# The first stage of a spectral-mixing and GeGLU kernel: where the layer norm's statistics, tile 13, the reciprocal roots and the angle tables are done

## The chip, the cores and the metric

The program runs on one core of one Trainium2 chip. A core has five engines with an instruction queue each: TensorE (PE in the profile, with PEld for its weight loads), VectorE (DVE), ScalarE (ACT), GpSimd (POOL) and SyncE (SP), which issues most DMAs. Each engine takes its own instructions strictly in the order of its queue and waits on semaphores for the others. The metric is the device time of one execution in microseconds (us), lower is better, given as the median of several runs.

## The reference

One input `x` of 2048 rows by 576 columns goes through two residual blocks:

```python
x  = A_x
h  = x + irfft2(rfft2(layernorm(x)) * (w_r + 1j * w_i))     # over both axes
h2 = h + (gelu(layernorm(h) @ w_gate) * (layernorm(h) @ w_up)) @ w_down
```

`layernorm` subtracts the mean over the 576 columns and divides by the root of the variance plus 1e-5. `w_r` and `w_i` are 2048 x 289, `w_gate` and `w_up` 576 x 4608, `w_down` 4608 x 576. Inputs and output are bf16.

## The kernel before, in words

The 2048 rows lie as 16 tiles of 128 rows (`h_sb[:, h, :]`, h = 0 to 15), loaded by six DMAs (tiles 0-1, 2-3, 4-5, 6-7, 8-11, 12-15). The Fourier transforms are matrix products with tables of sines that the kernel makes itself. The second block, the feed-forward part (lines 876 to 910), is one long run of matrix products from about 73 us to the end. This case is about the first stage, the first 34 us or so.

The order on every engine is written out by hand: the program sits under `tc.manual_schedule()`, so each engine gets its instructions in the order of the source text. Waits between engines are put in where data or buffers need them.

The first stage does the following, and the names are those of the code:

- **Statistics of a tile.** Even tiles and tile 15 have theirs on DVE, `sd(h)` (L117 to L119): `bn_stats` over each half of 288 columns, then `bn_aggr`, which makes mean and variance of the two. Tiles 1, 3, 5, 7, 9, 11 and 13 have theirs on ACT, `ln_act(h)` (L124): two passes over the tile with an accumulated sum, one for the mean and one for the mean square. `ln_fin` (L128, L129, POOL) makes a variance of the latter.
- **Reciprocal roots.** `ln_rstd` (L133, L134) on POOL, for four tiles at a time: add 1e-5, then raise to the power -0.5.
- **Normalise and transform.** `norms(lo, hi)`: for each tile DVE writes `xn` (L137, one `tensor_scalar`), and `row16(h)` has PE multiply it with the row table `F16` (L298; for tiles up to 11 also L311, which tiles 12 to 15 do together later). `fill` (L286) is PE work without use, ahead of tiles 0, 8 and 12 (14, 8 and 5 matmuls of 512 columns).
- **Evictions.** `evict(h)` (L322) copies two tiles' products from PSUM to `Bt` on ACT; 14 and 15 go one by one. `evict4(h)` (L328) copies four tiles' last columns, on ACT, and for tiles 12 to 15 on DVE. Large PSUM tiles come from a ring of four (`two`).
- **Column tables.** `phases` (L268) and `drop_sign(kd, pd)` (L223) on DVE make the angles of the table `DT`; `col_sin(1, pd)` and `col_sin(0, kd)` (L347) on ACT take their sines. `DF` is cleared by POOL (L387) and filled from `DT` by two DVE copies (L427, L428).
- **Middle tables.** `angle_a` (L236), `angle_b` (L246, L247) and `angle_c` (L223) on DVE, then `sine` (L253) and `cosine` (L256) on ACT, `minus_sine` (L259) on DVE, make the table `TF`. It is done in two parts: `first` (2 of 9 blocks, 256 columns) and `rest` (7 blocks, 896 columns). A transposing DMA turns `TF` into `TI`.
- **On POOL beside this**: two gathering DMAs of the spectral weights, `wm_r` and `wm_i` (L381), and the clearing of `DI` (L399) and of three tiles `Zt` (L401).

Then the second stage begins: `f2(c)` on PE (L478) multiplies `Bt` with `DT` and `DF`, ACT copies the product out as `pq` (L486; for c = 9 DVE does), `f3` (L493, L494) multiplies `pq` with `TF`, ACT copies `g` and `hs` (L514), and DVE makes sums `xab` (L523, L524), products with the weights (L541, L547, L548) and `Zt` (L552, L553), which PE's `i3` (L569, L571) takes. This repeats for eight values of k. On ACT's queue `sine(rest)` stands ahead of the copy of the first `pq`.

Of the kernel before, what the change touches and what calls it, by code (L numbers as in the profile page):

```python
# [9 lines left out]
ACT = mybir.ActivationFunctionType  # L10
# [31 lines left out]
def kernel_body(  # L42
# [143 lines left out]
    iota(q16[:], [[16, P]])  # L186
# [10 lines left out]
    for t in range(3):  # L197
# [10 lines left out]
    fs = tmp("fs", [P, P], FP32)  # L208
    A.activation(
        fs[:], mu[:].rearrange("p c l -> p (c l)"), ACT.Sin, bias=npib[:], scale=2.0 * PI / P  # L210
    )
    ia, s2a, s2p = tmp("ia", [P, 1]), tmp("s2a", [P, 1], FP32), tmp("s2p", [P, 1], FP32)
    V.tensor_scalar(ia[:], ip[:], 7, None, op0=ALU.bitwise_and)
    V.tensor_scalar(s2a[:], ia[:], 127.0 / 8.0, None, op0=ALU.mult)
    V.scalar_tensor_tensor(s2p[:], ip[:], 0.125, s2a[:], op0=ALU.mult, op1=ALU.add)
    ks = tmp("ks", [P, 9], FP32)
    V.tensor_scalar(ks[:], kv[:], s2p[:, 0:1], None, op0=ALU.mult)
    V.tensor_scalar(iu[:], iu[:], 7, None, op0=ALU.bitwise_and)
    mask = tmp("mask", [P, P], FP32)
    V.tensor_scalar(mask[:], iu[:].rearrange("p c l -> p (c l)"), 0.0, None, op0=ALU.is_equal)  # L220
# [24 lines left out]
    def angle_b(sl):  # L245
        V.tensor_scalar(pr[:, sl], pr[:, sl], 2047, None, op0=ALU.bitwise_and)  # L246
        V.tensor_scalar(ab[:, sl], pr[:, sl], -1024.0, None, op0=ALU.add)  # L247
# [18 lines left out]
    def phases():  # L266
        for t in range(3):
            V.scalar_tensor_tensor(  # L268
                pd[:, t, :], iJ[:], iD[:, t : t + 1], kd[:, t, :], op0=ALU.mult, op1=ALU.add
            )  # L270

    def row_table():
        V.tensor_tensor(
            F16[:, 0:2, :],
            fs[:].unsqueeze(1).to_broadcast([P, 2, P]),
            mask[:].unsqueeze(1).to_broadcast([P, 2, P]),
            ALU.mult,
        )
        V.tensor_scalar(F16[:, 2, :], F16[:, 0, :], -1.0, None, op0=ALU.mult)
# [8 lines left out]
    def row16(h):  # L288
        if h % 2 == 0 or h == H - 1:
            ps_f[h] = two("f2t")  # L290
        if h % 4 == 0:
            ps_f["f4", h] = two("f4")
        f2t, b = (ps_f[h], 0) if h in ps_f else (ps_f[h - 1], 1)
        fill(f2t[:, b, :], {0: 14, 8: 8, 12: 5}.get(h, 0))
        x = xn[:, h, :]
        for t in range(2):
            for n, d0 in ((0, t * P), (1, DH + t * P)):
                T.matmul(  # L298
                    f2t[:, b, t * 2 * P : (t + 1) * 2 * P],
                    lhsT=x[:, d0 : d0 + P],  # L300
                    rhs=F16[:, n : n + 2, :],
                    start=(n == 0),
                    stop=(n == 1),
                )
        if h < 12:
            row16_rest(h)
# [25 lines left out]

    def sd(*hs):
        for h in hs:
            ln_dve(mv, h)
# [24 lines left out]
    sd(2)  # L360
    ln_fin(slice(1, 4, 2))
    ln_rstd(rstd, mv, 0, 4)
    sd(4, 6)
    norms(0, 4)
# [9 lines left out]
    angle_a(first)  # L374
    angle_b(first)
    angle_c(first)
    sine(first)
# [9 lines left out]
    G.memset(DF[:], 0.0)  # L387
    ln_fin(slice(9, 12, 2))
    sd(8, 10)
# [3 lines left out]
    ln_act(13)  # L393
    sd(12, 14)
    norms(8, 12)
    sd(15)
    ln_fin(slice(13, 14))
    ln_rstd(rstd, mv, 12, 16)
# [248 lines left out]
    for i in range(n + 1):  # L647
# [3 lines left out]
        if i == 0:  # L651
            f2(order[0] + 8)
            angle_c(rest)
            minus_sine(rest)
# [307 lines left out]
```

## Time and profile before

| what | time |
|---|---|
| median of 3 runs | 503.44 us (503.3 to 503.62) |
| the profiled execution | 503.36 us |
| its span in the profile | 501.3 us |
| PE busy | 491.3 us, 98% of the span |
| DVE busy | 211.3 us, 42% |
| ACT busy | 152.6 us, 30% |
| POOL busy | 28.5 us, 6% |

The span runs from the first to the last instruction; the 2.06 us between it and the execution's own time lie around the program. A line of the timeline gives the start in us from the span's beginning, the busy time, engine, source line, operation, the output `<-` inputs with shapes, how many instructions were merged, and in brackets the idle time before it with what ended it. On DVE a following instruction that needs nothing of the one before starts a little before that one's recorded end; one that does need it starts about 0.03 us after the end. PE is nearly full over the whole span, but the first 34 us are where its holes are.

### The profile page before, as it was taken

The numbers are of one execution on the slowest core, as the hardware profiler recorded it, in microseconds if no ns is written. First come the engines' busy times: TensorE is split into PE (matmuls) and PEld (weight loads), VectorE is DVE, ScalarE is ACT, GpSimd is POOL, SyncE is SP. The second block draws the span as 40 slices with busy tenths as digits, with TensorE's granted clock in tenths as the row PEclk, the third lists the DMA queues.
The fourth block names the chain that finished last, engine by engine and source line by source line (L and its number), as shares of the span: only waits on it lengthen the run. The fifth ranks groups of instructions, "written<-read, shape, count | busy, mean of one in ns | idle before, by whom it ended". The sixth has DMA issues, their size and how long they took to land.

```text
span 501.3 us, 9901 instructions
## 1 busy us (share of the span) xinstructions
PE 491.3 (98%) x4340; PEld 290.9 (58%) x4340; DVE 211.3 (42%) x420; ACT 152.6 (30%) x269; POOL 28.5 (6%) x75
## 2 busy tenths in 40 slices
PE   7999999999999999999999999999999999999996
PEld 3567765555567754444477744444677544444775
DVE  8999766788640125433310145333210233333001
ACT  8999972222320012323200032333100133232000
POOL 8500010111110000000000000000000000000000
PEclk9999999999999999999999999999999999999999
DMA  8539686799950049998800099988300688870000
GB/s 283 172 72 198 183 236 160 152 168 189 178 102 1 1 107 184 193 190 155 158 9 0 7 210 203 195 159 151 74 0 1 144 159 159 154 143 1 12 13 26
DMA packets 88104, 61.46 MB, mean 123 GB/s; under 512 B 22781, under 2 KB 86653, under 8 KB 88061
## 3 DMA queue, kind: packets, MB, share of 16 engines
q1 hardware_dynamic: 87773, 59.65, 60.2%
q0 software_dynamic: 288, 1.18, 0.7%
q8 instruction: 34, 0.56, 0.5%
q14 instruction: 9, 0.07, 0.0%
HBM read 52.65 MB, written 2.36 MB: 110 GB/s over the span
## 4 chain that ended last, share of the span: by engine, by line
PE 93%; DVE 3%; ACT 2%; POOL 1%; issue 0%; POOLq 0%
PE gu L876 56%; PE acc L896 28%; PE cs_ps L618 2%; PE pq_ps L478 2%; PE y_ps L741 1%; PE eo_ps L571 1%; PE eo_ps L569 1%; PE gh_ps L494 1%; DVE xn L137 1%; ACT cwb L631 1%; PE gh_ps L493 1%; PE f2t L298 0%; ACT DT L347 0%; ACT Bt L322 0%; POOL kd L198 0%
## 5 line engine op out<-in xcount | busy, mean ns | idle before, releaser
L876 PE MATMUL gu<-Bt,wgu 64*128 64x512 bf16 x2592 | 281.5, 376 | 0.8 <-ACT cwb L631 0.8
L876 PEld LDWEIGHTS <-wgu 64*128 64x128 bf16 x2592 | 130.9, 94 | 148.2 <-issue 1.8
L884 ACT ACTIVATE g_sb<-gu 128x512 f32<-128x512 f32 x144 | 86.0, 597 | 302.8 <-PE gu L876 302.8
L885 DVE TENSOR_TENSOR P_sb<-g_sb,gu 128x512 bf16<-128x512 f32 x144 | 98.6, 685 | 152.9 <-ACT g_sb L884 152.9
L896 PEld LDWEIGHTS <-P_sb 128*128 128x128 bf16 x1152 | 112.4, 98 | 30.6 <-issue 2.4
L896 PE MATMUL acc<-wd,P_sb 128*128 128x288 bf16 x768 | 99.3, 286 | 0.0
L908 DVE TENSOR_TENSOR h_sb<-h_sb,acc 128x576 bf16<-128x576 bf16 x15 | 11.3, 754 | 118.2 <-PE acc L896 118.2
L896 PE MATMUL acc<-wd_a,P_sb 128*128 128x288 bf16 x384 | 52.3, 286 | 0.5 <-DVE h_sb L904 0.5
L478 PE MATMUL pq_ps<-DT,Bt 128*128 128x290 bf16 x64 | 12.2, 286 | 0.0
L286 PE MATMUL f2t<-h_sb,ident 128*128 128x512 bf16 x27 | 8.6, 479 | 3.7 <-DMA h_sb<-in_A_x_dram 3.7
L766 DVE TENSOR_SCALAR hrow<-h_sb,mv,rstd 128x1152 bf16<-128x1152 bf16 x14 | 12.1, 866 | 0.0
L134 POOL TENSOR_TENSOR rstd<-rstd,mhalf 128x1 f32<-128x1 f32 (+1 forms) x16 | 11.4, 713 | 1.3
L618 PEld LDWEIGHTS <-EO 128*128 128x128 bf16 x96 | 9.1, 96 | 3.0 <-issue 0.2
L478 PEld LDWEIGHTS <-Bt 128*128 128x128 bf16 x96 | 9.3, 97 | 2.4
L486 ACT CAST pq<-pq_ps 128x580 bf16<-128x580 f32 x15 | 9.8, 662 | 0.4 <-PE pq_ps L478 0.2
L133 POOL TENSOR_SCALAR rstd<-mv 128x1 f32<-128x1 f32 (+1 forms) x16 | 3.8, 238 | 107.3 <-DVE mv L119 107.0
L298 PE MATMUL f2t<-F,xn 128*128 128x256 bf16 x64 | 9.3, 275 | 0.7 <-DVE xn L137 0.7
L124 ACT ACTIVATE junk<-h_sb 128x576 bf16<-128x576 bf16 x14 | 9.4, 676 | 0.5 <-DMA h_sb<-in_A_x_dram 0.5
L118 DVE BATCH_NORM_STATS2 st<-h_sb 128x6 f32<-128x288 bf16 x21 | 9.3, 441 | 0.0
L117 DVE BATCH_NORM_STATS2 st<-h_sb 128x6 f32<-128x288 bf16 x21 | 9.3, 441 | 0.0
L618 PE MATMUL cs_ps<-DI,EO 128*128 128x290 bf16 x32 | 9.1, 285 | 0.0
L493 PE MATMUL gh_ps<-pq,TF 128*128 128x289 bf16 x32 | 8.7, 286 | 0.3 <-ACT TF L256 0.3
(132 smaller groups left out, 248.8 us busy)
## 6 DMA issues: line engine op xcount, KB each, us to landing
wgu<-in_B_w_gate_dram SPq DMA_DIRECT2D x48, 432.0 KB, 5.3
wgu<-in_B_w_up_dram SPq DMA_DIRECT2D x48, 432.0 KB, 6.8
wd<-in_B_w_down_dram SPq DMA_DIRECT2D x2, 1728.0 KB, 7.5
wd_a<-in_B_w_down_dram SPq DMA_DIRECT2D x1, 1728.0 KB
out_dram<-h_sb SPq DMA_DIRECT2D x3, 576.0 KB, 3.4
h_sb<-in_A_x_dram SPq DMA_DIRECT2D x4, 288.0 KB, 3.2
h_sb<-in_A_x_dram SPq DMA_DIRECT2D x2, 576.0 KB, 6.3
WR<-in_A_w_r_dram SPq DMA_DIRECT2D x1, 650.2 KB
```

What stands on the lines that cost most here:

```text
L124: A.activation(junk[:], h_sb[:, h, :], fn, scale=sc, accum_out=mv[:, h, i : i + 1])
L134: G.tensor_tensor(dst[:, sl], dst[:, sl], mhalf[:, sl], ALU.pow)
L478: T.matmul(ps[:, par, 0:JP], lhsT=Bt[:, t, col], rhs=DT[:, t // 2, par] if t < 4 else DF[:, par], start=(t == par), stop=(t == 4),)
L486: (V.tensor_copy if c == 9 else A.copy)(sb[:].rearrange("p r (j a) -> p r j a", a=2), ps[:, :, 0:JP].rearrange("p a (r j) -> p r j a", r=2),)
L493: T.matmul(dst, lhsT=TF[:, ts[k1], t0, :], rhs=a, start=True, stop=False)
L618: T.matmul(ps[:, e, 0:JP], lhsT=EO[x][:, 2 * e + jt if jt < 2 else 4, 2 * g : 2 * g + 2].rearrange("p h e k l -> p (h e k l)"), rhs=DI[:, ...
L766: V.tensor_scalar(hrow[:], h_sb[:, h, :].rearrange("p (r k) -> p r k", k=64).unsqueeze(2).to_broadcast([P, NR, 2, 64]), mv2[:, h, 0:1], rs ...
L876: T.matmul(gu[:, c, :], lhsT=w[rows, r, i * P : (i + 1) * P], rhs=hl[tcnk % 2][rows, r, :], start=(r == 0), stop=(r == NR - 1),)
L884: A.activation(g_sb[:], gu[:, 0, :], ACT.Gelu_apprx_tanh)
L885: V.tensor_tensor(p_sb(fa + i), g_sb[:], gu[:, 1, :], ALU.mult)
L896: T.matmul(acc[:, c, 0:DH], lhsT=p_sb(f)[:, st * P : (st + 1) * P], rhs=wd[f // NWA][:, f % NWA, cc], start=(f == 0), stop=(f == NFT - 1),)
L908: V.tensor_tensor(hv, hv, acc[:, :, 0:DH], ALU.add)
```

## The change

Nothing of the result changes. The parts, with the new lines:

1. `sd` writes the two halves' statistics, and the `bn_aggr` of a tile comes between the halves of the next tile (`flush`), or where `flush()` stands.
2. Tile 13's statistics are made on DVE (`sd(13)`); its `ln_act` and `ln_fin` go. Tiles 8, 10, 12 and 13 are done ahead of `xn` of tile 8, tiles 14 and 15 after `xn` of tile 13.
3. The reciprocal roots of tiles 12-15 become two calls, 12-13 and 14-15, and `xn` of 12 and 13 comes ahead of the statistics of 14 and 15.
4. `angle_a(first)` and `angle_b(first)` go ahead of `xn` of tile 0; the rest of the early angles, `angle_s` (which was the second half of `angle_b`) and `angle_c`, go among `xn` of tiles 0 to 3. `angle_a(rest)` is cut in two pieces (3 and 4 blocks) around the last `evict4` and the copies of `DF`; `angle_s(rest)` follows the copy of `pq` for c = 9; `minus_sine(rest)` follows the first sums `xab`.
5. `phases`: one of three instructions ahead of the last aggregate, `drop_sign(kd)` behind `xn` of tiles 14 and 15 instead of ahead of 12 to 15. `evict(12)` goes ahead of the two `col_sin`, `evict(14)` between them.
6. POOL clears `DF` after the roots of 12-13 instead of before those of 8-11.
7. The fills become 14, 2 and 3 (ahead of tiles 0, 8 and 14).
8. `row_table` is one DVE instruction instead of two, its mask is gone, and ACT makes the sines in two calls; `s2p` and `ks` take two DVE instructions fewer.

```diff
-    A.activation(
-        fs[:], mu[:].rearrange("p c l -> p (c l)"), ACT.Sin, bias=npib[:], scale=2.0 * PI / P
-    )
+    for n, bias, sign in ((slice(0, 2), npib, 1.0), (slice(2, 3), pib, -1.0)):
+        A.activation(fs[:, n], ..., ACT.Sin, bias=bias[:], scale=sign * 2.0 * PI / P)
...
     def angle_b(sl):
         V.tensor_scalar(pr[:, sl], pr[:, sl], 2047, None, op0=ALU.bitwise_and)
+
+    def angle_s(sl):
         V.tensor_scalar(ab[:, sl], pr[:, sl], -1024.0, None, op0=ALU.add)
...
     def row_table():
-        V.tensor_tensor(F16[:, 0:2, :], fs (twice), mask (twice), ALU.mult)
-        V.tensor_scalar(F16[:, 2, :], F16[:, 0, :], -1.0, None, op0=ALU.mult)
+        V.scalar_tensor_tensor(F16[:], iu (three times), 0.0, fs[:], op0=ALU.is_equal, op1=ALU.mult)
...
-        fill(f2t[:, b, :], {0: 14, 8: 8, 12: 5}.get(h, 0))
+        fill(f2t[:, b, :], {0: 14, 8: 2, 14: 3}.get(h, 0))
...
+    agg = []
+
+    def flush():
+        while agg:
+            h, st = agg.pop()
+            V.bn_aggr(mv[:, h, :], st[:])
+
     def sd(*hs):
         for h in hs:
-            ln_dve(mv, h)
+            st = roll.tile([P, 2, 6], FP32, name="st", tag="st", bufs=3)
+            V.bn_stats(st[:, 0, :], h_sb[:, h, 0:DH])
+            flush()
+            V.bn_stats(st[:, 1, :], h_sb[:, h, DH:D])
+            agg.append((h, st))
...
-    sd(2)
+    sd(2, 4)
     ln_fin(slice(1, 4, 2))
     ln_rstd(rstd, mv, 0, 4)
-    sd(4, 6)
-    norms(0, 4)
+    sd(6)
+    angle_a(first)
+    flush()
+    angle_b(first)
+    norms(0, 2)
+    angle_s(first)
+    norms(2, 4)
...
-    angle_a(first)
-    angle_b(first)
     angle_c(first)
+    sd(8)
     sine(first)
     cosine(first)
     norms(4, 8)
...
-    G.memset(DF[:], 0.0)
+    sd(10, 12)
     ln_fin(slice(9, 12, 2))
-    sd(8, 10)
     ln_rstd(rstd, mv, 8, 12)
     evict(4, 6)
     evict4(4)
-    ln_act(13)
-    sd(12, 14)
-    norms(8, 12)
-    sd(15)
-    ln_fin(slice(13, 14))
-    ln_rstd(rstd, mv, 12, 16)
+    sd(13)
+    norms(8, 9)
+    flush()
+    ln_rstd(rstd, mv, 12, 14)
+    G.memset(DF[:], 0.0)
+    norms(9, 14)
+    sd(14, 15)
+    phases(0)
+    flush()
+    ln_rstd(rstd, mv, 14, 16)
+    phases(1, 2)
     G.memset(DI[:], 0.0)
     for z in Zts:
         G.memset(z[:, :, J:], 0.0)
-    phases()
-    drop_sign(kd[:], pd[:])
     evict(8, 10)
     evict4(8)
+    evict(12)
     col_sin(1, pd, zerob)
+    norms(14, 16)
+    drop_sign(kd[:], pd[:])
+    minus_sine(first)
+    evict(14)
     col_sin(0, kd, hpib)
-    norms(12, 16)
-    minus_sine(first)
+    evict(15)
...
     for h in range(12, 16):
         row16_rest(h)
-    evict(12, 14, 15)
-    angle_a(rest)
+    angle_a(slice(2, 5))
+    evict4(12)
     V.tensor_copy(DF[0:32], D3[0:32])
     V.tensor_copy(DF[96:128], D3[96:128])
-    evict4(12)
+    angle_a(slice(5, 9))
     angle_b(rest)
...
+            angle_s(rest)
             angle_c(rest)
-            minus_sine(rest)
             weights()
...
                 sums_of(order[0])
+                minus_sine(rest)
```

More of the change, by code (lines that the diff above doesn't have):

```diff
@@ L185, in kernel_body @@
     q16 = tmp("q16", [P, P], FP32)
-    iota(q16[:], [[16, P]])
+    iota(q16[:], [[2, P]])
     make_identity(nc, ident[:])
@@ L207, in kernel_body @@
     V.tensor_scalar(mu[:], mu[:], 127, None, op0=ALU.bitwise_and)
-    fs = tmp("fs", [P, P], FP32)
-    A.activation(
-        fs[:], mu[:].rearrange("p c l -> p (c l)"), ACT.Sin, bias=npib[:], scale=2.0 * PI / P
-    )
[L212 to L215, printed above, removed]
+    fs = tmp("fs", [P, 3, P], FP32)
+    for n, bias, sign in ((slice(0, 2), npib, 1.0), (slice(2, 3), pib, -1.0)):
+        A.activation(
+            fs[:, n],
+            mu[:].rearrange("p c l -> p (c l)").unsqueeze(1).to_broadcast([P, n.stop - n.start, P]),
+            ACT.Sin,
+            bias=bias[:],
+            scale=sign * 2.0 * PI / P,
+        )
+    V.tensor_scalar(iu[:], iu[:], 7, None, op0=ALU.bitwise_and)
+    s2p = tmp("s2p", [P, 1], FP32)
+    V.scalar_tensor_tensor(s2p[:], iu[:, 0, 0:1], 127.0, ip[:], op0=ALU.mult, op1=ALU.add)
     ks = tmp("ks", [P, 9], FP32)
[L217 to L220, printed above, removed]
+    V.tensor_scalar(ks[:], kv[:], s2p[:, 0:1], 0.125, op0=ALU.mult, op1=ALU.mult)
     def drop_sign(dst, src):
@@ L264, in turn_tf, with phases @@
         )
-    def phases():
-        for t in range(3):
+    def phases(*ts):
+        for t in ts:
             V.scalar_tensor_tensor(
@@ L272, in row_table @@
     def row_table():
[L273 to L277, printed above, removed]
+        V.scalar_tensor_tensor(
+            F16[:],
+            iu[:].rearrange("p c l -> p (c l)").unsqueeze(1).to_broadcast([P, 3, P]),
+            0.0,
+            fs[:],
+            op0=ALU.is_equal,
+            op1=ALU.mult,
         )
-        V.tensor_scalar(F16[:, 2, :], F16[:, 0, :], -1.0, None, op0=ALU.mult)
     ps_f = {}
```

## The prediction, made before the changed kernel was run

> **What bounds the kernel now.** I read the page first, then the busy time by stages, the chain of waits between 19 and 35 us, and the timelines of DVE, ACT and POOL.
>
> The page, for the whole:
>
> ```profile
> span 501.3 us, 9901 instructions
> PE 491.3 (98%) x4340; PEld 290.9 (58%) x4340; DVE 211.3 (42%) x420; ACT 152.6 (30%) x269; POOL 28.5 (6%) x75
> PEclk9999999999999999999999999999999999999999
> ```
>
> PE is 98% busy, so the change can only act through the few holes at the start. Busy time by stages (us of PE, PEld, DVE, ACT, POOL):
>
> ```profile
> 9.10:16.95 7.85, 7.66 (x58) 4.05 (x57) 7.61 (x25) 7.84 (x17) 5.94 (x10) 1.00 0.96 289
> 16.95:25.11 8.16, 7.44 (x60) 4.26 (x61) 7.94 (x20) 7.80 (x13) 3.31 (x8) 1.00 0.43 120
> 25.11:27.38 2.27, 2.27 (x19) 1.74 (x19) 1.82 (x3) 2.20 (x4) 0.00 (x0) 1.00 0.15 27
> 33.80:55.00 21.20, 21.13 (x175) 16.33 (x174) 20.89 (x46) 19.62 (x36) 0.00 (x0) 1.00 1.08 217
> ```
>
> Up to 25 us DVE and ACT are both full, and PE's busy time includes useless fills. From 33.8 us DVE and PE are both full; what arrives late there stays late to the end. The chain goes through ACT:
>
> ```profile
> 19.76 1.01 ACT Bt L322
> 21.14 1.95 ACT DT L347 x2
> 23.09 0.90 ACT Bt L322
> 25.11 2.40 PE pq_ps L478 x18
> ```
>
> But the chain shows one of two that tie. The timelines of DVE and ACT:
>
> ```profile
> 13.74 0.41 DVE L117 BATCH_NORM_STATS2 st<-h_sb 128x6 f32<-128x288 bf16 x1
> 14.06 0.44 DVE L118 BATCH_NORM_STATS2 st<-h_sb 128x6 f32<-128x288 bf16 x1
> 14.54 0.21 DVE L119 BATCH_NORM_AGGREGATE mv<-st 128x2 f32<-128x12 f32 x1
> ...
> 16.51 1.40 DVE L137 TENSOR_SCALAR xn<-h_sb,mv,rstd 128x576 bf16<-128x576 bf16 x4
> ...
> 20.87 1.73 DVE L137 TENSOR_SCALAR xn<-h_sb,mv,rstd 128x576 bf16<-128x576 bf16 x4
> ...
> 25.09 0.63 DVE L246 TENSOR_SCALAR pr<-pr 128x896 int32<-128x896 int32 x1
> ```
>
> ```profile
> 25.75 1.04 ACT L253 ACTIVATE TF<-pr,pib 128x896 bf16<-128x896 int32 x1
> ```
>
> DVE has no idle time from 8.61 to 26.4. Its `angle_b(rest)` ends at 25.72; 0.03 later ACT starts `sine(rest)`, which stands ahead of the first `pq` copy (26.70); `f3` follows at 27.38. **So the DVE work ahead of 25.09 sets the end as much as ACT does.** And POOL:
>
> ```profile
> 13.67 0.59 POOL L387 MEMSET DF<- 128x580 bf16 x1
> 14.22 0.20 POOL L128 TENSOR_TENSOR sq<-mv 128x2 f32<-128x2 f32 x1
> ...
> 15.23 1.05 POOL L134 TENSOR_TENSOR rstd<-rstd,mhalf 128x4 f32<-128x4 f32 x1
> ...
> 20.58 0.75 POOL L399 MEMSET DI<- 128x580 bf16 x1
> ```
>
> A root of four takes 1.05, whenever its input comes. Where a clearing ran beside `xn`, four `xn` took 1.73 instead of 1.40.
>
> **The change, step by step, along DVE.** Start-to-start times of the rows: an `xn` 0.34; a tile of statistics 0.92 (13.74 to 14.66), interleaved 0.37 + 0.13 + 0.32 = 0.82, since an aggregate no longer waits for the half just before it.
>
> *Up to xn of tile 0: nothing.* POOL's queue as far as the root that releases it (8.61) keeps its order. ACT's longer sines (0.4 more) lie in its 0.49 idle ahead of 3.69. DVE ahead of it: statistics of tile 0 from 3.70, 0.74; the one-piece `row_table` about 0.53 (384 columns on the line from 0.48 for 256 to 1.14 for 896, less the overlap of 0.08); three tiles, 2.46; early `angle_a`, aggregate, `angle_b`, about 0.8: 8.2 us. If tile 6 lands as late as it was read before (7.43), this is 0.4 late; the 0.6 idle below takes that up, so it costs nothing either way.
>
> GPSIMD Engine Reference of the Trainium skill (section 1, Specifications) says that GpSimd shares its SBUF interfaces with VectorE, with contention against VectorE instructions of two SBUF inputs. That speaks against `angle_a` beside the root at 7.53; but the root at 9.89 had `angle_a` beside it and took 1.06, no longer than the others. By the rule the sum would be up to 0.48 higher, by the row 0; I take the row.
>
> *To xn of tile 8: 0.89 earlier than its 16.51, limited by POOL.* DVE: 8.61, four `xn`, two early angle steps (0.22, 0.27), tile 8's halves 0.74, four `xn`: 12.56; tiles 10, 12, 13: 15.02. POOL: the gathers end at 13.67 as before, and without the `DF` clearing the four steps (0.28 + 0.28 + 0.31 + 1.05) give the root at 15.59. `xn` of tile 8 starts at 15.62; DVE idles 0.60.
>
> *To xn of tile 12.* Tile 13's aggregate ends at 16.17; POOL adds from 16.27 (0.33) and takes a root of two. No row has it: 0.57 for one, 1.05 for four; I take 0.73, on the line between, ends 0.57 and 1.05. `xn` of tile 12: 17.36; DVE was free at 17.12, 0.24 idle.
>
> *To xn of tile 14.* The `DF` clearing now starts as that root ends, beside `xn` of 12 and 13. Price between 0 and 0.33 (1.73 - 1.40); I take 0.33, since a clearing of the same 580 columns made it. Then two `xn` 0.68, tile 14 0.74, tile 15 0.82, one of `phases` 0.42: 20.35. Aggregate to 20.56, POOL add from 20.66, root to 21.72: `xn` of 14 at 21.75, against 21.85 before, when 12 and 13 were done as well. DVE idles 0.41, the rest of `phases` (0.86) and the aggregate hiding the rest of the wait.
>
> *To angle_b(rest).* Two `xn` with the clearing of `DI` beside them (0.68 + 0.33): 22.76. Then `drop_sign(kd)`, 0.53, which stood ahead of tile 12 before; `minus_sine(first)` 0.14; the two `angle_a` pieces (384 and 512 columns, 0.53 and 0.75 + 0.03, the second now right ahead of its user), the `CAST` 0.61, `DF` copies 0.54: `angle_b(rest)` at 25.89, against 25.09: **0.80 later**. What is gained (early angles, 0.83, moved into the wait for POOL; cheaper aggregates) is outweighed by 1.25 of new idle, tile 13 (0.82) and a clearing beside `xn` twice instead of once.
>
> *ACT and PE: nothing gained.* Tile 13 took 1.34 of ACT (17.17 to 18.51). But `col_sin(0)` now waits for `drop_sign(kd)` (23.4), and the last eviction ends near 24.96 as before; `f2` starts at about 25.1. The fills taken away (8 of 0.22) lie where PE waits for `xn`.
>
> *On to the loop.* `sine(rest)` 26.55, first `pq` 27.50, `f3` 28.18 (+0.80). Its second matmul waited 0.11 for DVE's `pq` before (27.61), and not now: +0.69. `minus_sine(rest)` (0.42) now lies between the sums and the products: 0.34 in the queue, less the 0.12 that the products waited for the sums, 0.21. `Zt` is **0.90 later**, and the loop behind it has no slack. Its reader, the second `f3`, meets it within 0.1.
>
> DMAs: the transposing one of `first` moves 0.8 later on SP, and the six small copies behind it with it; their first reader is at 33.8. The second one still waits for `cosine(rest)`, later than `minus_sine`; the weight loads behind it are first read at 72.6. Covered.
>
> **Sum:** 503.36 + 0.90 = 504.26; this execution stood 0.08 below the median, so 504.3 us. Ends: no cost beside the clearings (-0.66) and roots at 0.57 (-0.32) give 503.4; roots at 1.05 (+0.64), aggregates of 14 and 15 not hidden (+0.2), `drop_sign(kd)` slowed by the clearing of `Zt` (+0.2) give 505.4.
>
> **Rivals.** I call 0.2%, 1 us, what a measurement tells from no change.
>
> *A. The chain is right and ACT was the bound* (faster side). Then POOL's roots come before DVE asks for them: the 1.25 idle goes, 504.34 - 1.25 = 503.1 us; with clearings that cost nothing, 502.4. For it: the chain's lines, and 1.34 us off ACT. Against it: the root's 1.05 and the 0.33 of add and issue come from rows. It decides from 0.9 us less waiting. 13%.
>
> *B. The upper ends hold:* POOL's two short roots cost what a long one costs, or more is lost beside the clearings: 504.5 to 505.4. For it: the root at 19.46 took 1.38, not 1.05, beside `drop_sign`. Against it: a root of one is 0.57. 28%.
>
> *C. PE's clock falls.* PE waits about 1.6 us ahead of tile 14, with few fills. Fourteen fills took 5.41 us cold, eight 1.90 warm; a cold stretch that long beside full work costs some 2 us: 506. The page's clock shows no drop. TensorE: Matmul & The Clock Gate of the Trainium skill (Part 1) puts the fall after an idle window of about 3.4 us; by that rule, no drop here, and no run here shows one. 2%.
>
> The forecast has 57%, 503.4 to 504.5 its own range. **Range 502.9 to 505.2**, which leaves the far ends of A, B and all of C out. Below 502.43 only the best of A: faster 5%; the forecast, most of A and the lower edge of B: same 65%; slower 30%.
>
> **What the profile after would show.** Right: `xn` of tile 0 at 8.6 and of tile 8 near 15.6, DVE idle with POOL's root as releaser ahead of tiles 8, 12 and 14; roots of two near 0.73; `xn` of 12 to 15 long beside clearings; `sine(rest)` released by DVE near 26.5; `f2` near 25.1 and PE idle ahead of `f3` near 28.2; the first 512-column product of the feed-forward part 0.9 later. Wrong: no idle ahead of tiles 8 and 14, or `sine(rest)` before 25.75.

## The result, and the profile after

The changed kernel took **505.44 us** (median of 6 runs, 504.9 to 505.56); the kernel before, run beside it, 503.37 (503.19 to 504.62, 6 runs). The ratio is 1.0035, 95% interval 1.0025 to 1.0045: slower by 2.07 us. I had forecast 504.3, with 505.2 as the upper end, so the sign was right and the size too small: 0.9 us forecast, 2.07 measured. In the experiments below, four executions of 646 to 1828 us, one of them of the kernel before, are left out.

In the profiled executions (of the changed kernel the longest of its six, 505.56) the span grew from 501.3 to 503.4 us. The first 512-column product of the feed-forward part starts at 74.42 instead of 72.59, 1.83 later, and the last PE matmul is 1.83 later as well (499.54 against 497.71): 1.74 of this is there when `angle_b(rest)` starts (below), and nothing came back. The other 0.2 us of the span lie behind the issue of the last store, where the change moves nothing. The page of the changed kernel:

```profile
span 503.4 us, 9878 instructions
PE 490.0 (97%) x4330; PEld 290.2 (58%) x4332; DVE 211.4 (42%) x420; ACT 152.0 (30%) x266; POOL 29.2 (6%) x75
PEclk9999999999999999999999999999999999999999
```

DVE's work is the same to 0.1 us, ACT has 0.6 less, PE's clock is full. So it is a matter of order. The busy time by the stages of the prediction (PE, PEld, DVE, ACT, POOL, then clock and DMA):

```profile
9.10:16.95 7.85, 7.00 (x54) 3.84 (x54) 6.88 (x23) 7.42 (x17) 6.00 (x10) 1.00 0.90 259
16.95:25.11 8.16, 6.18 (x53) 3.52 (x51) 7.29 (x20) 6.66 (x9) 3.96 (x9) 1.00 0.36 117
25.11:27.38 2.27, 1.97 (x18) 1.32 (x17) 2.19 (x5) 1.28 (x4) 0.00 (x0) 1.00 0.69 105
```

DVE was busy 7.61 and 7.94 us in the first two stretches before; now it is 6.88 and 7.29, so 1.38 us of idle time have come into the engine that is needed most. Its timeline says where, and for whom it waits:

```profile
11.44 1.64 DVE L137 TENSOR_SCALAR xn<-h_sb,mv,rstd 128x576 bf16<-128x576 bf16 x4 [0.21 <-POOL rstd L134]
...
16.21 0.43 DVE L137 TENSOR_SCALAR xn<-h_sb,mv,rstd 128x576 bf16<-128x576 bf16 x1 [0.76 <-POOL rstd L134]
...
18.00 1.00 DVE L137 TENSOR_SCALAR xn<-h_sb,mv,rstd 128x576 bf16<-128x576 bf16 x2 [0.27 <-POOL rstd L134]
...
22.48 1.10 DVE L137 TENSOR_SCALAR xn<-h_sb,mv,rstd 128x576 bf16<-128x576 bf16 x2 [0.61 <-POOL rstd L134]
23.50 0.68 DVE L225 TENSOR_SCALAR kd<-pd 128x870 int32<-128x870 int32 x1
...
25.39 0.30 DVE L455 COPY DF<-DT 32x580 bf16<-32x580 bf16 x1
25.71 0.31 DVE L456 COPY DF<-DT 32x580 bf16<-32x580 bf16 x1
26.05 0.75 DVE L238 SCALAR_TENSOR_TENSOR pr<-q,s2p,ks 128x512 int32<-128x512 f32 x1
26.83 0.63 DVE L248 TENSOR_SCALAR pr<-pr 128x896 int32<-128x896 int32 x1
```

Behind `xn` of tile 0 there are four waits, all for POOL's roots, where before there was none. The first, 0.21 ahead of tile 4, costs nothing by itself, since DVE waits for POOL ahead of tile 8 again. The three ahead of tiles 8, 12 and 14 make 1.64 us. `angle_b(rest)` (the last line) starts at 26.83 instead of 25.09. ACT and PE show what follows from it:

```profile
27.49 1.04 ACT L257 ACTIVATE TF<-pr,pib 128x896 bf16<-128x896 int32 x1 [1.10 <-DVE pr L248]
```

```profile
23.20 1.05 PE L303 MATMUL f2t<-F,xn 128*128 128x256 bf16 x8 [1.93 <-DVE xn L137]
```

`sine(rest)` is now released by DVE after ACT has stood idle for 1.10; before, it started right behind `angle_b` too, but ACT had been busy nearly up to it. `f3` starts at 29.11 instead of 27.38. POOL, whose roots DVE waits for:

```profile
9.34 0.33 POOL L129 TENSOR_TENSOR mv<-mv,sq 128x2 f32<-128x2 f32 x1 [0.54 <-ACT junk L124]
9.75 0.29 POOL L133 TENSOR_SCALAR rstd<-mv 128x4 f32<-128x4 f32 x1
10.13 1.27 POOL L134 TENSOR_TENSOR rstd<-rstd,mhalf 128x4 f32<-128x4 f32 x1
11.61 1.37 POOL L403 DMA_INDIRECT wm_r<-in_A_w_r_dram,rev  x1 [0.21 <-issue]
13.28 0.95 POOL L403 DMA_INDIRECT wm_i<-in_A_w_i_dram,rev  x1 [0.30 <-issue]
...
15.13 1.04 POOL L134 TENSOR_TENSOR rstd<-rstd,mhalf 128x4 f32<-128x4 f32 x1
...
17.23 0.73 POOL L134 TENSOR_TENSOR rstd<-rstd,mhalf 128x2 f32<-128x2 f32 x1
...
21.61 0.83 POOL L134 TENSOR_TENSOR rstd<-rstd,mhalf 128x2 f32<-128x2 f32 x1
```

The first short root takes 0.73, as estimated, the second 0.83. But the gathers end at 14.24, where they ended at 13.67 before, though nothing in POOL's queue up to there has been moved. The same stretch before:

```profile
9.27 0.19 POOL L129 TENSOR_TENSOR mv<-mv,sq 128x2 f32<-128x2 f32 x1 [0.53 <-ACT junk L124]
9.55 0.26 POOL L133 TENSOR_SCALAR rstd<-mv 128x4 f32<-128x4 f32 x1
9.89 1.06 POOL L134 TENSOR_TENSOR rstd<-rstd,mhalf 128x4 f32<-128x4 f32 x1
11.17 1.24 POOL L381 DMA_INDIRECT wm_r<-in_A_w_r_dram,rev  x1 [0.21 <-issue]
12.71 0.96 POOL L381 DMA_INDIRECT wm_i<-in_A_w_i_dram,rev  x1 [0.30 <-issue]
```

### The profile page after: what moved, and what is told of

It reads as the page before. It is cut to its first block, busy times and chain, and to the rows that moved or that the text cites. A ratio compares the mean times of both kernels' runs of the same rounds, so it can differ in the third digit from the quotient of the medians.

```text
span 503.4 us, 9878 instructions
## 1 busy us (share of the span) xinstructions
PE 490.0 (97%) x4330; PEld 290.2 (58%) x4332; DVE 211.4 (42%) x420; ACT 152.0 (30%) x266; POOL 29.2 (6%) x75
## 4 chain that ended last, share of the span: by engine, by line
PE 91%; DVE 3%; ACT 2%; POOL 1%; issue 1%; DMA 1%; POOLq 0%
PE gu L905 56%; PE acc L925 28%; PE cs_ps L646 2%; PE pq_ps L506 1%; PE y_ps L770 1%; ACT junk L124 1%; PE eo_ps L599 1%; POOL rstd L134 1%; PE eo_ps L597 1%; PE gh_ps L522 1%; PE gh_ps L521 1%; ACT cwb L659 1%; DMA h_sb<-in_A_x_dram 1%; DVE xn L137 1%; POOL wm_r L403 0%
## 5 line engine op out<-in xcount | busy, mean ns | idle before, releaser
L134 POOL TENSOR_TENSOR rstd<-rstd,mhalf 128x1 f32<-128x1 f32 (+2 forms) x17 | 11.8, 694 | 1.4
L291 PE MATMUL f2t<-h_sb,ident 128*128 128x512 bf16 x18 | 7.3, 571 | 3.8 <-DMA h_sb<-in_A_x_dram 3.8
L133 POOL TENSOR_SCALAR rstd<-mv 128x1 f32<-128x1 f32 (+2 forms) x17 | 4.2, 247 | 110.4 <-DVE mv L119 106.8
L506 PE MATMUL pq_ps<-DF,Bt 128*128 128x290 bf16 x32 | 8.9, 284 | 0.0
L327 ACT CAST Bt<-f2t 128x1024 bf16<-128x1024 f32 (+1 forms) x9 | 8.2, 921 | 1.9 <-PE f2t L303 1.9
L597 PE MATMUL eo_ps<-TI,Zt 128*128 128x256 bf16 x35 | 8.7, 272 | 0.0
```

What stands on the lines that cost most here:

```text
L134: G.tensor_tensor(dst[:, sl], dst[:, sl], mhalf[:, sl], ALU.pow)
L506: T.matmul(ps[:, par, 0:JP], lhsT=Bt[:, t, col], rhs=DT[:, t // 2, par] if t < 4 else DF[:, par], start=(t == par), stop=(t == 4),)
L597: T.matmul(pv[:, n], lhsT=z[:, o : o + P], rhs=TI[:, ts[k], 1:3, :], start=True, stop=False)
```

## The experiments

Each was timed beside the kernel before (its medians there: 503.63, 503.51, 503.63 and 503.55). The changed kernel was not run again, so kernels are compared by how far their median lies over that of the kernel before beside them; for the changed kernel that is 2.07 us. My theory: DVE's queue up to `angle_b(rest)` sets the end, and the loss is DVE's waits for POOL's roots. The rivals: ACT's chain sets the end; the split into two roots costs by itself; the fewer fills cost through PE's clock.

### Fills alone

```diff
-        fill(f2t[:, b, :], {0: 14, 8: 8, 12: 5}.get(h, 0))
+        fill(f2t[:, b, :], {0: 14, 8: 2, 14: 3}.get(h, 0))
```

> The kernel before with only the fills of the change (14, 2 and 3 matmuls ahead of tiles 0, 8 and 14 instead of 14, 8 and 5 ahead of 0, 8 and 12). Theory (VectorE's queue ahead of angle_b(rest), with its waits for GpSimd's roots, makes the loss): no more than 0.1 us over the kernel before, since PE waits for xn there anyway: 503.4 to 503.5. Rival (the fewer fills leave TensorE idle and its clock or its row products late): most of the loss comes back, 504.5 or more.

Measured: 505.64 us, ratio 1.0040 (1.0027 to 1.0053). My theory, that fills cost nothing, failed. The mean clock was 0.993 to 0.997 in every run. The windows of the profiled one, 3.41 us each (PE's busy time stands behind the comma, its clock is the first of the last three numbers):

```profile
17.27:20.68 3.41, 2.95 (x24) 1.68 (x24) 3.38 (x11) 3.41 (x7) 0.69 (x3) 1.00 0.74 241
20.68:24.09 3.41, 0.69 (x7) 0.62 (x8) 2.45 (x6) 3.41 (x5) 2.73 (x6) 1.00 0.03 10
24.10:27.51 3.41, 3.41 (x15) 1.76 (x12) 1.98 (x5) 1.60 (x2) 0.00 (x0) 0.50 0.35 67
```

```profile
23.41 1.27 PE L298 MATMUL f2t<-F,xn 128*128 128x256 bf16 x8 [2.81 <-DVE xn L137]
24.46 1.49 PE L286 MATMUL f2t<-h_sb,ident 128*128 128x512 bf16 x3
```

After a hole of 2.81 us PE ran at half clock from 24.10 to 27.51, just where it had four tiles to catch up: three fills took 1.49 us instead of 0.82. So the fills of the kernel before are not idle work, they hold the clock. But this is not where the changed kernel lost: its clock was 1.00 in the profiled run and in four of the five others, and the fifth (0.995) took 505.4, no longer than they did. The next two runs split the fills further.

### Which fills

```diff
-        fill(f2t[:, b, :], {0: 14, 8: 8, 12: 5}.get(h, 0))
+        fill(f2t[:, b, :], {0: 14, 8: 8, 14: 3}.get(h, 0))     # five_fills_moved_alone
+        fill(f2t[:, b, :], {0: 14, 8: 2, 12: 5}.get(h, 0))     # six_fills_alone
```

> The kernel before with only the fills of PE ahead of tile 12 changed: 14, 8 and 3 ahead of tiles 0, 8 and 14 instead of 14, 8 and 5 ahead of tiles 0, 8 and 12. Theory (the hole of PE ahead of tile 12 grows from under 2 us to near 2.8 us, and that is what let the clock fall in the run with all three fills changed): a mean clock under 1 in most runs and 505 to 507 us. Rival (the six fills that were taken away ahead of tile 8 are what matters): clock 1, and 503.5 us, at most 0.2 above the kernel before for the three fills that now stand between tile 13 and tile 14.

Measured: 503.79 us, 1.0014 (1.0000 to 1.0029), and two kinds of run: seven at 503.49 to 504.27 with clock 1.000, four at 505.81 to 506.51 with clock 0.997. I had expected the fall in most runs. The same program loses its clock in some runs and in others not; where it does, the time lies 2.2 us or more above the median of the seven.

> The kernel before with only the six fills taken away that stood ahead of tile 8: 14, 2 and 5 ahead of tiles 0, 8 and 12. Theory (the clock is set anew every 3.41 us and falls where PE was busy for a third of such a stretch or less; ahead of tile 8 PE waits some 1.1 us of what were 1.9 us of fills, so no stretch comes under 60%): a mean clock of 1 in all runs and the time of the kernel before, 503.4 to 503.7. Rival (fewer fills lower the clock wherever they are taken away): a mean clock under 1 in some runs, and these at 505 or more.

Measured: 503.73 us (median of eleven), 1.0003 (0.9994 to 1.0012). Theory failed again, in part: the time is that of before, but two runs lost the clock (504.41 with 0.997 and 504.55 with 0.996). Two others took as long without a fall (504.63 and 504.70, clock 0.999), as three runs of the kernel before beside them did. The profiled run (504.41) shows the fall:

```profile
14.61:18.02 3.41, 1.92 (x15) 0.95 (x14) 3.34 (x12) 3.41 (x8) 1.37 (x3) 1.00 0.79 276
18.02:21.43 3.41, 3.41 (x18) 1.38 (x16) 3.27 (x9) 2.08 (x4) 2.65 (x6) 0.50 0.50 153
```

The clock fell after a stretch with PE busy 1.92 of 3.41 us (56%). The changed kernel came through a stretch with 1.49 (44%) unharmed:

```profile
19.95:23.37 3.42, 1.49 (x12) 0.81 (x10) 2.81 (x9) 2.98 (x4) 2.14 (x6) 1.00 0.05 14
```

So a threshold of the busy share is not the rule, or not the whole of it; this stays open. What the runs do show is that the four falls that are in a profile came a whole number of 3.41 us stretches (3, 4 or 5) after the clock's rise and lasted one of them, and that the rise itself moves between 7.09 and 10.44 us from profile to profile. The fall costs less here (the feed-forward part of the profiled run starts 1.06 later than in the kernel before) than with tiles 12 to 15 behind it: PE had until 20.9 us, when `xn` of tile 12 was due, to catch up.

### Tile 14's statistics in the wait

```diff
-    sd(13)
+    sd(13, 14)
     norms(8, 9)
...
-    sd(14, 15)
+    sd(15)
     phases(0)
```

> The changed kernel with tile 14's statistics moved ahead of xn of tile 8, into VectorE's 0.76 us of waiting for the root of tiles 8 to 11. Theory: xn of tile 8 stays at 16.2, the 0.76 of idle goes, the wait ahead of tile 12 (0.27) goes with it, since tile 13's aggregate is earlier, the wait ahead of tile 14 stays: sine(rest) from 27.5 to about 26.4, the time 1.1 us shorter, 504.3. Rival (ScalarE's evictions or TensorE's row products set the end): within 0.2 of the changed kernel, 505.4.

Measured: 504.29 us, 1.0017 (1.0008 to 1.0026); 0.66 over the kernel before, so 1.4 of the 2.07 us are gone, where the theory had 1.1. The two groups of `xn` in this run:

```profile
15.86 0.41 DVE L137 TENSOR_SCALAR xn<-h_sb,mv,rstd 128x576 bf16<-128x576 bf16 x1
...
21.07 1.10 DVE L137 TENSOR_SCALAR xn<-h_sb,mv,rstd 128x576 bf16<-128x576 bf16 x2 [0.61 <-POOL rstd L134]
```

With 0.8 us of work put where DVE had waited, the wait ahead of tile 8 is gone, and `xn` of tile 14 comes 1.41 earlier; 1.36 of that reach the feed-forward part (73.06 instead of 74.42). Time on DVE passes to the end nearly one to one. But 0.35 of the 1.41 are not the edit's: POOL's gathers ended at 13.80 in this run, so `xn` of tile 8 came at 15.86 instead of 16.21. The other 1.06 are what the theory had: the waits ahead of tiles 8 and 12 gone, the one ahead of tile 14 as it was.

### minus_sine(rest) back

```diff
             angle_s(rest)
             angle_c(rest)
+            minus_sine(rest)
             weights()
...
                 sums_of(order[0])
-                minus_sine(rest)
```

> The changed kernel with minus_sine(rest) back ahead of the weights, where it was before. Theory: the sums wait for ScalarE's hs anyway (0.56 us idle ahead of them), so it is free there, while between sums and products it costs 0.21: 0.2 us shorter than the changed kernel, 505.2. Rival (the loop behind has slack): 0.

Measured: 505.09 us, 1.0034 (1.0021 to 1.0047), 1.46 over the kernel before: 0.6 less than the changed kernel, with an interval that takes in 0.2 as well as nothing. The profile tells more. `angle_b(rest)` started 0.29 earlier by itself in this run (26.54), as POOL had been quicker; the move shows behind it. In this run the products come 0.87 us after the start of the first sums (30.73 to 31.60), in the changed kernel 1.09 (31.02 to 32.11), so 0.22 for the 0.42 us instruction between them.

### Tile 13 on DVE alone

```diff
-    ln_act(13)
-    sd(12, 14)
+    sd(12, 13, 14)
...
-    ln_fin(slice(13, 14))
```

> The kernel before with only tile 13's statistics moved from ACT to DVE (between those of tiles 12 and 14). Theory (DVE's queue sets the masked angles of the rest, and with them the end): 0.93 us more in its queue, less 0.1 to 0.2 us of waits that it fills; the time 504.2 to 504.5. Rival (ACT's chain of evictions and sines sets the end, and it gets 0.76 us shorter): no slower than before, 503.5 or less. Should the later tile 12 open a hole of PE that lets its clock fall: 505 or more with a mean clock under 1.

Measured, on the kernel before: 504.10 us, 1.0011 (1.0002 to 1.0020; eleven runs within 0.16 us), which is 0.47 over the kernel before by the medians, a little less than expected. In the profiled runs the feed-forward part starts 0.88 later.

```profile
17.46 1.40 DVE L137 TENSOR_SCALAR xn<-h_sb,mv,rstd 128x576 bf16<-128x576 bf16 x4
...
26.02 0.63 DVE L246 TENSOR_SCALAR pr<-pr 128x896 int32<-128x896 int32 x1
```

No wait was there to be filled: `xn` of tile 8 is 0.95 later, `angle_b(rest)` 0.93, the start of the feed-forward part 0.88. ACT had 1.3 us less to do, and it did not help. With that the rival that ACT sets the end (A in the prediction) is out.

### The aggregates alone

```diff
-            ln_dve(mv, h)
+            st = roll.tile([P, 2, 6], FP32, name="st", tag="st", bufs=3)
+            V.bn_stats(st[:, 0, :], h_sb[:, h, 0:DH])
+            flush()
+            V.bn_stats(st[:, 1, :], h_sb[:, h, DH:D])
+            agg.append((h, st))
...
-    sd(8, 10)
+    sd(8, 10, 12)
...
-    sd(12, 14)
-    norms(8, 12)
+    sd(14)
+    norms(8, 9)
+    flush()
+    norms(9, 12)
     sd(15)
+    phases(0)
+    flush()
```

> The kernel before with only the aggregates put behind the next tile's first half (tile 13 stays on ACT, one root of four for tiles 12 to 15, angles where they were; the first of the phases stands ahead of the last aggregate, as in the changed kernel). Theory (DVE's statistics get 0.12 us shorter a tile, and it waits that much more for POOL's roots): idles of DVE ahead of xn of tiles 8 and 12, 0.3 to 0.5 us each, eat what six tiles save, and the time stays within 0.3 us of before, 503.5. Rival (the saving reaches the end, since DVE's queue has next to no idle in the kernel before): some 0.5 to 0.8 us faster, 502.8.

Measured: 503.98 us, 1.0007 (0.9999 to 1.0016): not faster. (Its profiled run, 504.66, was the longest of eleven, so the waits in it may be longer than in the others.) Each tile's statistics take 0.8 instead of 0.92 us, and DVE waits instead:

```profile
16.38 0.43 DVE L137 TENSOR_SCALAR xn<-h_sb,mv,rstd 128x576 bf16<-128x576 bf16 x1 [0.46 <-POOL rstd L134]
...
21.57 2.10 DVE L137 TENSOR_SCALAR xn<-h_sb,mv,rstd 128x576 bf16<-128x576 bf16 x4 [0.93 <-POOL rstd L134]
```

What is won on DVE arrives at roots that are not ready.

### One root again, alone

```diff
-    ln_rstd(rstd, mv, 12, 14)
     G.memset(DF[:], 0.0)
-    norms(9, 14)
+    norms(9, 12)
     sd(14, 15)
     phases(0)
     flush()
-    ln_rstd(rstd, mv, 14, 16)
+    ln_rstd(rstd, mv, 12, 16)
...
-    norms(14, 16)
+    norms(12, 16)
```

(with `evict(12)` behind `xn` again, and the three late fills ahead of tile 12)

> The changed kernel with only the split of the rstds undone: one addition and one root for tiles 12 to 15, behind the statistics of tile 15 as the second root stands now, and tiles 12 and 13 normalised with 14 and 15; the two late fills go ahead of tile 12 again (14, 2, 3 ahead of tiles 0, 8, 12). Theory (what costs is that DVE waits for the last root with little left to do, not that there are two): xn of tile 12 starts near 21.3 us after a wait of 0.8, all four take 1.7 to 1.9 us beside the clearing, the masked angles of the rest start near 27.0 instead of 26.8, and the kernel takes 505.6 us, within 0.3 of the changed one. Rival (the split itself is the loss, 0.73 and 0.83 us of root and twice the addition against one of 1.2): near 504.5 us.  Should PE's clock fall in its longer hole ahead of tile 12 (2 us or more), 506 to 508 with a mean clock under 1.

Measured: 506.23 us (median of five), 1.0060 (1.0047 to 1.0073), 2.6 over the kernel before: 0.5 us worse than the changed kernel, where I expected 0.2. Two of the five lost PE's clock (506.50 and 507.69); the profiled one, 506.23, did not. The rival that the split is the loss is out.

```profile
21.51 1.95 DVE L137 TENSOR_SCALAR xn<-h_sb,mv,rstd 128x576 bf16<-128x576 bf16 x4 [0.94 <-POOL rstd L134]
...
26.05 0.30 DVE L454 COPY DF<-DT 32x580 bf16<-32x580 bf16 x1 [0.54 <-ACT DT L365]
```

`xn` of tile 12 waits 0.94, nearly as expected. The rest is of my own making: I had left `evict(12)` and `evict(14)` ahead of `col_sin(0)` on ACT, they wait for PE's four tiles, and the `DF` copies wait 0.54 for `col_sin(0)`. Without that `angle_b(rest)`, at 27.48, would lie 0.1 from the changed kernel's 26.83. So the split shows no cost of its own; how much it helps, this run doesn't settle.

### No waits: one root, and two roots

Both have the statistics of tiles 13 and 14 ahead of `xn` of tile 8, `phases` and `drop_sign(kd)` ahead of the last group of `xn`, and `angle_a(rest)` in one piece, with `angle_b(rest)` ahead of the last `evict4` and the `DF` copies; `angle_s(rest)` follows these, and `minus_sine(rest)` stands where it was before. They differ in the roots and, with them, in the places of the late fills, of the clearing of `DF` and of the last evictions. Against the changed kernel, the core of the second:

```diff
-    sd(13)
+    sd(13, 14)
     norms(8, 9)
...
-    sd(14, 15)
+    sd(15)
     phases(0)
...
+    drop_sign(kd[:], pd[:])
+    col_sin(0, kd, hpib)
     norms(14, 16)
-    drop_sign(kd[:], pd[:])
     minus_sine(first)
     evict(14)
-    col_sin(0, kd, hpib)
...
-    angle_a(slice(2, 5))
+    angle_a(rest)
+    angle_b(rest)
     evict4(12)
     V.tensor_copy(DF[0:32], D3[0:32])
     V.tensor_copy(DF[96:128], D3[96:128])
-    angle_a(slice(5, 9))
-    angle_b(rest)
+    angle_s(rest)
...
```

> The changed kernel reordered so that VectorE does not wait for a root after tile 8: tile 13 and 14 ahead of xn of 8, tile 15 behind xn of 11, one root for tiles 12 to 15, phases and drop_sign(kd) ahead of xn of 12, then angle_a and angle_b(rest) ahead of the last evict4 and the copies of DF, angle_s(rest) and minus_sine(rest) where they were before; fills 14, 2, 3. Tile 13, the interleaved aggregates and the early angles stay as changed. Theory: sine(rest) can start at about 25.4 right behind ScalarE's G16, f3 near 27.1, the time 2.2 us below the changed kernel and 0.3 below the kernel before: 503.1. Rival (tile 13 on VectorE or the few fills make the loss): 504.5 or more.

Measured: 503.68 us (median of eleven), 1.0005 (0.9996 to 1.0014), 0.05 over the kernel before: the loss is gone, but the 0.3 below the kernel before that the theory promised did not come. One root of tiles 12 to 15 comes at 20.67 and DVE still waits 0.28 for it; PE then has four tiles at once, and `f2` starts at 25.18, no earlier than the 25.11 of before.

> The rstds of tiles 12-13 and 14-15 stay apart, as in the change, but both roots are asked for early: the statistics of tiles 13 and 14 stand ahead of xn of tile 8, that of tile 15 behind xn of tile 13, the phases and the drop of kd's sign ahead of xn of tile 14, the rest's masked angles ahead of the four-tile eviction and of the two DF copies; the first minus_sine and the angles of the first two rows as in one_root_no_waits; fills 14, 2, 3 ahead of tiles 0, 8, 14. Theory (the split costs only where DVE has nothing to do while POOL takes the second root): no idle of DVE ahead of xn of tiles 12 and 14, tile 12 on PE right behind tile 11, f2 near 24.8 us and the first gate matmul near 72.3, so about 503.2 us, some 2.2 us under the changed kernel and no slower than with one root. Rival (two short roots cost more than one long one whatever stands beside them, 2 x 1.15 us with the additions against 1.45): at least 0.5 us over the run with one root, 504.2 or more. A third way, PE idle for 2 us or more ahead of tile 14 and its clock falls: 505 or more, with a mean clock under 1.

Measured: **503.09 us, 0.9990 (0.9981 to 0.9999)**: 0.42 under the kernel before and so 2.5 us better than the changed one. Against the kernel before that is less than what I call a difference but with an interval that stays under 1. With two roots it is the faster one of the pair, by 0.5; as the pair differs in more than the roots, this is not the worth of the split.

```profile
16.25 0.43 DVE L137 TENSOR_SCALAR xn<-h_sb,mv,rstd 128x576 bf16<-128x576 bf16 x1 [0.19 <-POOL rstd L134]
16.60 0.20 DVE L343 BATCH_NORM_AGGREGATE mv<-st 128x2 f32<-128x12 f32 x1
16.72 2.08 DVE L137 TENSOR_SCALAR xn<-h_sb,mv,rstd 128x576 bf16<-128x576 bf16 x5
...
21.61 1.06 DVE L137 TENSOR_SCALAR xn<-h_sb,mv,rstd 128x576 bf16<-128x576 bf16 x2
```

`xn` of tile 8 is no earlier than in the changed kernel (16.25 against 16.21), since POOL's queue is the same. What counts is that the wait is 0.19 and not 0.76, and that tiles 12 and 14 wait for nothing: 1.45 us of waits are gone. `angle_b(rest)` starts at 23.89, which is 2.94 earlier than in the changed kernel; most of the rest is the eviction and the two `DF` copies (0.60 and 0.64 start to start), which now stand behind it. But the feed-forward part starts only 1.72 earlier (72.70). In this trace `f2` started at 25.17 and not at 24.8: the four-tile eviction stands behind `angle_b(rest)` on DVE, and PE waits 0.51 for it.

### The gathers behind the root

```diff
-    for t, w in zip(wm, (A_w_r, A_w_i)):
-        G.indirect_dma_start(...)
     sd(10, 12)
     ln_fin(slice(9, 12, 2))
     ln_rstd(rstd, mv, 8, 12)
...
     ln_rstd(rstd, mv, 12, 14)
+    for t, w in zip(wm, (A_w_r, A_w_i)):
+        G.indirect_dma_start(...)
     G.memset(DF[:], 0.0)
```

> The changed kernel with the two indirect gathers of the weights issued behind the root of tiles 12-13 instead of ahead of the additions and the root of tiles 8-11. Theory (POOL's queue, with the gathers in it, sets xn of tile 8, and what is won there reaches the end): the additions come when tile 10's statistics are in, xn of tile 8 starts some 0.4 us earlier, and so the first gate matmul, 74.0 instead of 74.4: 505.0 us. Rival (xn of tile 12 and 14 wait for their own roots, and these wait for DVE's statistics, so an earlier tile 8 is given back at tile 12 or 14): 505.4 as it is. Against both: the gathered weights come late for the first products at 29 to 30 us; they take some 3 us to land, so not expected.

Measured: 505.73 us, 1.0040 (1.0026 to 1.0054), 2.22 over the kernel before. The time is the rival's. `xn` of tile 8 comes 0.5 earlier, as the theory said, and that is given back further on:

```profile
15.71 0.43 DVE L137 TENSOR_SCALAR xn<-h_sb,mv,rstd 128x576 bf16<-128x576 bf16 x1 [0.43 <-POOL rstd L134]
...
22.08 1.43 DVE L137 TENSOR_SCALAR xn<-h_sb,mv,rstd 128x576 bf16<-128x576 bf16 x2 [0.93 <-POOL rstd L134]
```

The gathers and the clearing of `DF` now stand ahead of the second root, which starts late (its addition at 20.84, though tile 15's aggregate was done at 20.33, so it is POOL's queue and not, as the rival had it, DVE's statistics); the clearings of `DI` and `Zt` then fall wholly beside `xn` of tiles 14 and 15 (1.43). A fall of PE's clock came with it in four of the five runs, but the fifth, without one, took 505.70, so the fall isn't needed for the loss. The gathers took 4.8 and 5.5 us from issue to landing, not 3, and were still in time.

### The clearing moved

```diff
     G.memset(DF[:], 0.0)
+    G.memset(DI[:], 0.0)
+    for z in Zts:
+        G.memset(z[:, :, J:], 0.0)
     norms(9, 14)
...
-    G.memset(DI[:], 0.0)
-    for z in Zts:
-        G.memset(z[:, :, J:], 0.0)
```

> The changed kernel with the clearing of DI and of the Zt pads put right behind the clearing of DF, so that POOL clears nothing beside xn of tiles 14 and 15. Theory (POOL's clearing slows the normalisation on DVE beside it, as the prediction priced it): xn of tiles 14-15 takes 0.75 us instead of 1.10, angle_b(rest) comes 0.3 us earlier, and the kernel takes 505.1 us. Rival (the slower xn comes from PE or the evictions beside it, not from POOL): xn of tiles 14-15 stays at 1.1 us and the time at 505.4; what now stands beside the clearing, tiles 12-13 and tile 14's statistics, may lose what is won, up to 0.3 us.

Measured: 506.10 us, 1.0052 (1.0037 to 1.0066), 2.59 over the kernel before: 0.5 worse than the changed kernel instead of 0.3 better. Two of the six lost PE's clock; the median of the four others is 505.97. The mechanism is the one I named, at a price I had not thought of:

```profile
17.43 0.57 POOL L418 MEMSET DF<- 128x580 bf16 x1
...
17.51 1.94 DVE L137 TENSOR_SCALAR xn<-h_sb,mv,rstd 128x576 bf16<-128x576 bf16 x2 [0.27 <-POOL rstd L134]
...
17.95 0.57 POOL L419 MEMSET DI<- 128x580 bf16 x1
18.47 0.48 POOL L421 MEMSET Zt<- 128x124 bf16 x3
...
22.93 0.77 DVE L137 TENSOR_SCALAR xn<-h_sb,mv,rstd 128x576 bf16<-128x576 bf16 x2 [0.61 <-POOL rstd L134]
```

`xn` of tiles 14 and 15 takes 0.77 (it took 1.10), so that part came out. But `xn` of tiles 12 and 13 takes 1.94. Only the first of these two is long: it starts at 17.51, 0.08 after the first clearing has begun, takes 1.61 instead of 0.42 and ends at 19.12, 0.17 after the last of the five clearings, which follow each other without a gap. The second takes 0.41, as if alone. The other traces have the same 0.17: `xn` of tile 12 in the changed kernel (0.67) ends 0.17 after the one clearing beside it, and `xn` of tile 14 with the gathers behind the root (1.10) ends 0.17 after the last of four. So an `xn` that meets a clearing stands until POOL lets go. That isn't always the end of the row: in the changed kernel `xn` of tile 14 (0.66) came in between the clearing of `DI` and the first of `Zt`, which then took 0.36 instead of 0.19. What decides this stays open. SBUF — State Buffer of the Trainium skill (SBUF: two separate sides) says that VectorE, in its two-port modes, and GpSimd hold a shared port pair as an exclusive lock for a whole instruction, and the other one blocks; the trace agrees that the two did not share. Whether `xn` ran in such a mode no trace shows.

## Why the prediction was right or wrong, point by point

*What bounds the kernel: right.* "The DVE work ahead of 25.09 sets the end as much as ACT does": tile 13 alone put 0.93 on DVE and 0.88 on the start of the feed-forward part in its profiled run (0.47 on the median), though it took 1.3 us off ACT. Rival A fell with it; in the changed kernel ACT stands idle 1.10 ahead of `sine(rest)`.

*Up to xn of tile 0: right, with some luck (see GpSimd below).* 8.65 against 8.61.

*To xn of tile 8: the step that failed.* I had 15.62; it came at 16.21, 0.59 of the 0.94 that `angle_b(rest)` came later than forecast (26.83, not 25.89). That POOL limits it was right. DVE's wait there (0.76, forecast 0.60) is near only because DVE was 0.43 later than forecast as well (free at 15.45, not 15.02): the sum had no wait for the root of tiles 4 to 7, and it cost 0.21 ahead of tile 4. Wrong was "the gathers end at 13.67 as before". POOL's pieces from 9.34 to the gathers' end took 4.90 us instead of 4.40: start to start 0.13 more for the subtraction, 0.04 for the addition, 0.20 for the root, 0.13 for the first gather; and they started 0.07 later. I had kept the queue's order and taken the durations for granted ("a root of four takes 1.05, whenever its input comes", though the profile before has one of 1.38 at 19.46), while DVE had other work beside them. They vary, too: in the seven profiles with the changed order up to there the stretch took 4.57 to 4.98, in the six with the angles where they stood before (one of these with the aggregates interleaved) 4.34 to 4.45. The changed kernel's is one of the longest.

*To xn of tiles 12 and 14: right.* From one `xn` to the next 1.79 and 4.48 us, against 1.74 and 4.39. In the second, two misses offset each other: the addition and root on POOL took 0.24 more than forecast, DVE's work 0.13 less. The short roots took 0.73 and 0.83, for 0.73. Rival B's form, that two short roots cost what a long one costs, did not come true here. But in other kernels a short root took 0.95 (two roots, no waits) and 1.00 (tile 14's statistics in the wait), so it wasn't far.

*Beside the clearings: right in size, for the wrong reason.* 1.00 and 1.10 against 0.77 alone are 0.23 and 0.33, for 0.33 each. But it is no slowing by so much: the `xn` that meets a clearing stands until POOL lets go (0.67 and 0.66 for 0.42 in the two pairs, 1.61 with the clearing moved).

*To angle_b(rest): 0.21 short.* `drop_sign(kd)` took 0.61 start to start for 0.53, with the clearing of the `Zt` pads beside it, which I had only in the upper end. And the two `DF` copies took 0.66, for which I had 0.54; the rows of before give 0.65 (23.72 to 24.37), so that was a misreading.

*On to the loop: right.* From `angle_b` to the feed-forward part I had 0.10 more; it was 0.09 (1.74 and 1.83). `minus_sine(rest)` cost 0.22, for 0.21. `f2` started at 25.89 and not near 25.1, since tile 14 and `col_sin(0)` came later than forecast; `f3` waited for `sine(rest)` all the same.

*GpSimd beside angle_a: the row misled.* I took the row (1.06 at 9.89, no longer beside `angle_a`) over GPSIMD Engine Reference of the Trainium skill (section 1), for the root at 7.53. That root took 1.05 here as well. But in two later kernels with the same order up to there it took 1.35 and 1.36, and `xn` of tile 0 came at 8.96 and 8.97. The lines of one of them (`minus_sine(rest)` back):

```profile
7.55 0.46 DVE L238 SCALAR_TENSOR_TENSOR pr<-q,s2p,ks 128x256 int32<-128x256 f32 x1
7.57 1.35 POOL L134 TENSOR_TENSOR rstd<-rstd,mhalf 128x4 f32<-128x4 f32 x1
```

In both the root began 0.02 behind `angle_a`. Where it began 0.01 behind it (two roots, no waits) it took 1.05, and in the row I took, where the root had begun 0.09 ahead, 1.06. So the traces agree with the Trainium skill that `angle_a` can hold up a root, but whether it does hangs on hundredths of a microsecond. It cost nothing at tile 8, as POOL's next subtraction waited for ACT until 9.3 anyway. In the changed kernel it was the next root that was long, 1.27, beside DVE's `drop_sign` and the statistics of tile 8, and what stood ahead of it was longer too. That DVE's work is the cause there is argued, not shown: no run took that work away, and in the run with the clearing moved, with the same work beside it, the same root took 1.07. By the Trainium skill a loss at tile 8 could have been feared, not its size.

*Rival C and the fills: the reason was wrong.* "The fills taken away lie where PE waits for xn", so they cost nothing. In the changed kernel its clock stayed up in five of six runs, and the sixth was no slower, so rival C did not come true; PE waited 1.93 for 1.6. But it came close to the edge: the same fills in the order of before lost the clock in each of five runs. TensorE: Matmul & The Clock Gate of the Trainium skill (Part 1) gives a free-running window of about 3.4 us, and by the phase of the falls the traces agree; for the fall it gives an idle window of that length, and there the traces differ: holes of 1.49, 2.27 and 2.81 us did it. The measurement decides.

So the sum's DVE waits of 1.25 us came out at 1.64 and its start of the feed-forward part, 0.90 later, at 1.83: 0.59 of the difference is POOL's stretch ahead of the gathers' end. The end, 505.4, is where the upper bounds taken together had put it, on another ground; that is chance. What made POOL's stretch longer stays open.

## What to carry to other kernels

Work taken off a full engine is worth something only if what this engine waits for next comes earlier too: here each saving on DVE ended in a wait for POOL's root, until the statistics of a further tile were put into the wait. When a queue is moved against another engine's, take the other engine's durations as a range: here the same pieces took 4.34 to 4.45 us beside one order of DVE's work and 4.57 to 4.98 beside another. And useless matmuls that hold PE's clock should be weighed by the hole that they close, over several runs, before they are taken out.

## What the runs showed of the hardware that I had not expected

- PE's clock fell to half for 3.41 us after holes of PE of 1.49 to 2.81 us, in some runs of a program and not in others (in 5 of 5, 4 of 11 and 2 of 11 with other fills; with the changed kernel's fills in 1 of 6, and in 4 of 5 with the gathers behind the root); it fell 10.24, 13.65 or 17.07 us after its rise, whole multiples of 3.41. What decides within such a stretch stays open (56% busy fell, 44% did not).
- An `xn` of 128 x 576 that started 0.08 us after a clearing on POOL had begun took 1.61 us instead of 0.42: five clearings passed before it ended, 0.17 us after the last. The next `xn` took 0.41.
- A POOL root of 128 x 4 took 1.04 to 1.38 us, one of 128 x 2 took 0.72 to 1.00. Beside DVE's `angle_a` one of 128 x 4 took 1.35 and 1.36 when it began 0.02 us behind it, 1.05 at 0.01 us behind and 1.06 at 0.09 us ahead.
